# A fused sliding-window attention and mixer kernel: V of batch 1 ahead of the last quarter of w2, the four output sums of chunk 0 side by side, and unread matmuls between batch 0's values

## The chip, the cores and the metric

The kernel runs on one core of a Trainium2 chip. TensorE (PE, with its weight loads PEld) multiplies matrices into PSUM; VectorE (DVE), ScalarE (ACT) and GpSimd (POOL) work beside it, and SyncE (SP) issues transfers; POOL and ACT issue transfers too. The metric is the device time of one execution in microseconds. Lower is better.

## What is computed

Attention with a window of 64 over 8 batches, 8 heads, 576 positions and 64 dimensions a head; its output, laid out as (batch, position, 512), goes through a low-rank mixing of positions (U, V of rank 32) and a two-layer network with a relu. Types in and out are float32; the kernel computes in bf16 with float32 sums.

```python
scores = scale * np.matmul(q, k.transpose(0, 1, 3, 2))
mask = (rel >= 0) & (rel < window)            # rel = query position - key position
attn = softmax(np.where(mask, scores, -1e9))
x = np.matmul(attn, v)                        # then (B, S, H * D)
h = x.transpose(0, 2, 1) @ U @ V
u = x + h.transpose(0, 2, 1)
out = u + np.maximum(u @ w_ch1, 0.0) @ w_ch2
```

## The kernel before

**Work and tiles.** The 8 x 576 = 4,608 rows of u are cut into nine chunks of 512 rows for the network, while attention goes batch by batch. A chunk has 16 pieces `ch1(i)` (four matmuls of 128x512 into `psA`, then a relu on ScalarE or, for a few i, on VectorE) and 16 pieces `ch2(t, quarter)` (four matmuls of 128x512 into `psU`, the output sum of the 128 rows t; a quarter covers four of the sixteen row blocks of w2). After the last quarter of a t, the sum is added to u (line 683) and stored by SP. Each of these 32 pieces is the "fill" of one slot, 0 to 31.

Batch 0's attention runs alone, ahead of the loop. The attention of batch c + 1 is laid into the slots of chunk c: `KT` (transposes of K and Q on VectorE), `S` (scores on TensorE, exp on ScalarE at line 379, mask on VectorE at line 386), `VC` (copies that pair V's halves from `vA` into `vB`, lines 138 and 139), `PV` (values into `xr`, then reciprocal and multiply on VectorE, lines 417 and 427), `U` (into `pshh`, then a copy by ScalarE), `XT` and `UP` (the transposed u of the first two chunks, then four copies at line 551) and `V` (the addition of line 494). The tables `PLACE_1` and so on say which slot. In chunk 0, up to slot 20 the fill stands first and the slot's pieces behind it; from slot 21 on the pieces stand first. Within an engine everything runs in this written order.

**Order of the sums.** For chunk 0 the second layer goes by quarters over t = 0, 1, 2 and then takes t = 3 with all four quarters; other chunks go t by t.

**PSUM.** Pool `big` has two tiles of two banks, taken in turn by scores, values, U, XT and V. Pool `mm` has three tiles of one bank for `psA` and `psU`; pool `tp` has one tile of one bank, used for U of batch 1 only. In batch 0's stage a pool `x0` of two tiles stands in the place of `mm` and `tp`.

**Queues.** All loads from memory are issued by POOL, in this order around the change: w1 in three parts, w2 blocks 0 to 7, K and Q of batch 1 (four loads), w2 blocks 8 to 15, V of batch 1 (four loads into `vA`, one into `vB`), U for odd batches (two loads), then K and Q of batch 2 and V of batch 2 (lines 114 and 126 are the later batches' K, Q and V). The issues share eight completion semaphores in turn, so an issue waits until the eighth load before it has landed. SP stores the outputs and, with ACT and POOL, moves the transposed u of the later chunks.

**Unread matmuls.** `turn_over(n, cols)` multiplies a tile of zeros into a bank that nothing reads. It runs at the start, between score pieces of batch 0, and before chunk 0.

The lines that the change touches: 441 to 445 (bank of `pshh`), 671 and 672 (bank of a sum), 681 to 686 (emptying of a sum), 689 to 691 (order), `PLACE_1` (703 to 711), the loads (769 and 770) and batch 0's values (776 to 779).

Of the kernel before, what the change touches and what calls it, by code (L numbers as in the profile page):

```python
# [9 lines left out]
ALU = mybir.AluOpType  # L10

BF16 = mybir.dt.bfloat16
FP32 = mybir.dt.float32
# [3 lines left out]
def kernel(  # L17
# [11 lines left out]
    nc = tc.nc  # L29
# [93 lines left out]
    def load_v(b):  # L123
        va, vb = vA[b % 2], vB[b % 2]
        for t in range(NFULL):
            nc.gpsimd.dma_start(  # L126
                out=va[:, t, :, 0:D],
                in_=v[b, :, t * P : (t + 1) * P, :].rearrange("h p d -> p h d"),
            )
        nc.gpsimd.dma_start(  # L130
            out=vb[0:W, NFULL, :, 0:D],
            in_=v[b, :, NFULL * P : S, :].rearrange("h p d -> p h d"),
        )
# [65 lines left out]
    def load_w2(lo, hi):  # L199
        nc.gpsimd.dma_start(out=w2b[:, lo:hi, :], in_=w2v[:, lo:hi, :])  # L200
# [22 lines left out]
    def attention(b, alone=False):  # L223
# [213 lines left out]
        def UM(ts):  # L437
            def f():
                half = CH // 2
                if ts[0] == 0:  # L440
                    if b == 1:
                        hh["one"] = psum["tp"].tile([P, CH], FP32, name="pshh1", tag="tp")
                    else:
                        big = ps_big.tile([P, 2, CH], FP32, name="pshh", tag="big")
                        hh["one"] = big[:, 0, :]
                    if b < 2:
                        hh["ps"] = hh["one"].rearrange("p (n x) -> p n x", n=2)
                    else:
                        hh["ps"] = big[:, :, 0:half]
                ps = hh["ps"]  # L450
                for t in ts:
                    xt = x[:, t, :, :].rearrange("p h d -> p (h d)")
                    if b < 2:
                        nc.tensor.matmul(
                            hh["one"][t % 4 * R : (t % 4 + 1) * R, :],
                            ub[odd][:, t, :],
                            xt,
                            start=(t < 4),
                            stop=(t > 0),
                        )  # L460
                        continue
                    for n in range(2):
                        g = t if t < 4 else n
                        nc.tensor.matmul(
                            ps[g * R : (g + 1) * R, n, :],
                            ub[odd][:, t, :],
                            xt[:, n * half : (n + 1) * half],
                            start=(t < 4),
                            stop=(t != n),
                        )  # L470
                if ts[-1] == NT - 1:
                    hh["sb"] = wk_pool.tile([P, CH], BF16, name="hh", tag="hh")
                    nc.scalar.copy(out=hh["sb"].rearrange("p (n x) -> p n x", n=2), in_=ps)
            return f
# [133 lines left out]
    def mlp(c):  # L608
        uTc = uT_of(c)
        c1 = [None] * NFC  # L610

        psA0 = []

        def uT_cols(dc):
            cols = uTc[:, dc, :]
            if c < 2:
                return cols
            return cols.rearrange("p (i t q) -> p t i q", i=4, t=TPC)

        def ch1(i):  # L620
            def f():
                if c == 0 and i < 2:
                    if i == 0:
                        psA0.append(ps_big.tile([P, 2, CH], FP32, name="psA0", tag="big"))
                    ps = psA0[0][:, i, :]
                    todo = [(n, dc) for two in ((0, 2), (1, 3)) for n in range(2) for dc in two]
                else:
                    ps = psum["mm"].tile([P, CH], FP32, name="psA", tag="mm")[:]
                    todo = [(i, dc) for dc in range(NDC)]
                for n, dc in todo if c > 0 or i != 1 else ():  # L630
                    to = psA0[0][:, n, :] if c == 0 and n < 2 else ps
                    nc.tensor.matmul(  # L632
                        to if c < 2 else to.rearrange("p (t i q) -> p t i q", i=4, t=TPC),
                        w1b[:, dc, n * P : (n + 1) * P],
                        uT_cols(dc),
                        start=(dc == 0),
                        stop=(dc == NDC - 1),
                    )
                c1[i] = c1_pool.tile([P, CH], BF16, name=f"c1_{i}")
                if i in (DVE_RELU if c != 1 else (7, 10, 13)):  # L640
                    nc.vector.tensor_relu(out=c1[i][:], in_=ps)  # L641
                else:
                    nc.scalar.activation(out=c1[i][:], in_=ps, func=ACT.Relu)  # L643
            return f

        acc = {}

        def ch2(t, quarter):
            def f():
                g = c * TPC + t  # L650
                if c == NCH - 1 and t == TPC - 1:
                    if quarter % 2 == 0:
                        acc[t] = psum["mm"].tile([P, DM], FP32, name="psU", tag="mm")
                    cols = slice(quarter // 2 * (DM // 2), (quarter // 2 + 1) * (DM // 2))
                    for i in range(8 * (quarter % 2), 8 * (quarter % 2) + 8):
                        nc.tensor.matmul(  # L656
                            acc[t][:, cols],
                            c1[i][:, t * P : (t + 1) * P],
                            w2b[:, i, cols],
                            start=(i == 0),  # L660
                            stop=(i == NFC - 1),
                        )
                    if quarter % 2 == 1:
                        osb = out_pool.tile([P, DM], FP32, name="osb")
                        nc.vector.tensor_tensor(
                            out=osb[:, cols], in0=acc[t][:, cols], in1=u_tiles[g][:, cols], op=ALU.add
                        )
                        queue = nc.scalar if quarter == 1 else nc.sync
                        queue.dma_start(out=outf[g * P : (g + 1) * P, cols], in_=osb[:, cols])
                    return  # L670
                if quarter == 0:
                    acc[t] = psum["mm"].tile([P, DM], FP32, name="psU", tag="mm")
                for i in range(4 * quarter, 4 * quarter + 4):
                    nc.tensor.matmul(  # L674
                        acc[t][:],
                        c1[i][:, t * P : (t + 1) * P],
                        w2b[:, i, :],
                        start=(i == 0),
                        stop=(i == NFC - 1),
                    )  # L680
                if quarter == 3:
                    osb = out_pool.tile([P, DM], FP32, name="osb")
                    nc.vector.tensor_tensor(  # L683
                        out=osb[:], in0=acc[t][:], in1=u_tiles[g][:], op=ALU.add
                    )
                    nc.sync.dma_start(out=outf[g * P : (g + 1) * P, :], in_=osb[:])
            return f

        order = [(t, r) for t in range(TPC) for r in range(4)]
        if c == 0:  # L690
            order = [(t, r) for r in range(4) for t in range(3)] + [(3, r) for r in range(4)]
        return [ch1(i) for i in range(NFC)] + [ch2(t, r) for t, r in order]


# [7 lines left out]
    }  # L702
    PLACE_1 = {
        "KT": [11, 12, 14, 15],
        "S": [14, 14, 17, 17, 21, 21],
        "VC": [20, 21, 22, 23],
        "PV": [22, 23, 24, 25, 26],
        "U": [28],
        "XT": [28] * 4,
        "UP": [29],  # L710
    }
    PLACE_2 = {
        "V1": [0, 1, 17],
# [15 lines left out]
    def turn_over(n, cols=CH, to=None):  # L729
        for _ in range(n):  # L730
            nc.tensor.matmul(
                (unread if to is None else to)[:, 0, 0:cols],
                idle[:, 0:P],
                idle[:, 0:cols],
                start=to is None,
                stop=to is None,
            )
# [19 lines left out]
    for f in a["VC"][0:2]:  # L757
# [8 lines left out]
    load_w1(1024, 2048)  # L766
    load_w2(0, 8)
    load_kq(1)
    load_w2(8, 16)
    load_v(1)  # L770
    nc.gpsimd.dma_start(out=ub[1][W:P, 0, :], in_=moe_U[0:W, :])
    nc.gpsimd.dma_start(
        out=ub[1][:, 1:NT, :], in_=moe_U[W:S, :].rearrange("(c p) r -> p c r", p=P)
    )
    xT0 = [psum["x0"].tile([P, 2, CH], FP32, name=f"xT{i}", tag="x0") for i in range(2)]
    unread = xT0[0]
    a["PV"][2]()
    a["PV"][3]()
    a["PV"][4]()
    a["XT"][0]()  # L780
    for f in a["U"]:
# [95 lines left out]
```

## Time and profile before

| | us |
|---|---|
| median of four runs | 321.92 |
| lowest and highest of them | 320.49, 323.21 |
| the profiled execution's own time | 321.81 |
| its span, first to last instruction | 320.1 |
| TensorE matmuls busy, of the span | 308.9 (96%) |
| VectorE, ScalarE, GpSimd busy | 209.5, 106.1, 104.4 |

The profile is one execution. Busy time counts an engine's instructions, not its waits; matmuls overlap in the pipeline, so a busy TensorE isn't one at its peak. The clock row gives the share of full speed that TensorE was granted. Time outside the span (1.7 us here) belongs to the launch. Durations of one instruction that matter: a relu or copy of 128x512 out of PSUM on ScalarE, 597 ns; the sum's addition on VectorE, 671 ns; the exp of 128x768 on ScalarE, 811 ns; a copy of 64x520 on GpSimd, 616 ns, on ScalarE 621 to 625 ns, on VectorE some 290 ns. Matmuls of 128x512 start 0.216 us apart at full clock.

### The profile page before, as it was taken

The numbers are of one execution on the slowest core, as the hardware profiler recorded it, in microseconds if no ns is written. First come the engines' busy times: TensorE is split into PE (matmuls) and PEld (weight loads), VectorE is DVE, ScalarE is ACT, GpSimd is POOL, SyncE is SP. The second block draws the span as 40 slices with busy tenths as digits, with TensorE's granted clock in tenths as the row PEclk, the third lists the DMA queues.
The fourth block names the chain that finished last, engine by engine and source line by source line (L and its number), as shares of the span: only waits on it lengthen the run. The fifth ranks groups of instructions, "written<-read, shape, count | busy, mean of one in ns | idle before, by whom it ended". The sixth has DMA issues, their size and how long they took to land.

```text
span 320.1 us, 7020 instructions
## 1 busy us (share of the span) xinstructions
PE 308.9 (96%) x2879; PEld 152.1 (48%) x2905; DVE 209.5 (65%) x368; ACT 106.1 (33%) x174; POOL 104.4 (33%) x156
## 2 busy tenths in 40 slices
PE   8789998999999999999999999999999999999995
PEld 7554454455444544454444444444444444444444
DVE  7754948778797859778967795769577722412211
ACT  1544533275008320652065204630373004203400
POOL 8681428540059303930484038403000300030000
PEclk9979999999999999999999999999999999999999
DMA  7999999999359995999699939992400140050011
GB/s 118 160 194 206 207 152 165 206 194 126 28 144 165 161 79 131 146 167 124 147 168 175 85 62 192 184 131 38 165 0 2 41 158 0 0 166 33 2 66 67
DMA packets 108929, 38.05 MB, mean 119 GB/s; under 512 B 98352, under 2 KB 101808, under 8 KB 108896
## 3 DMA queue, kind: packets, MB, share of 16 engines
q0 software_dynamic: 92480, 25.63, 107.4%
q1 hardware_dynamic: 11232, 10.69, 10.1%
q10 hardware_dynamic: 5184, 1.28, 1.8%
q8 instruction: 23, 0.38, 0.5%
q14 instruction: 10, 0.08, 0.1%
HBM read 48.94 MB, written 9.44 MB: 182 GB/s over the span
## 4 chain that ended last, share of the span: by engine, by line
PE 61%; DMA 22%; POOL 6%; DVE 5%; issue 3%; SPq 2%; DVEq 0%; POOLq 0%
PE psA L632 27%; PE psU L674 26%; DMA vA<-in_v_dram 12%; DMA qr<-in_q_dram 5%; DMA w1b<-in_moe_w_ch_dram 3%; PE xr L408 2%; SPq L596 2%; PE sc L371 2%; POOL kr L114 2%; POOL qr L114 2%; DVE un L494 2%; PE psv L483 2%; DMA uTc<-stg 1%; DVE stg L570 1%; PE psU L656 1%
## 5 line engine op out<-in xcount | busy, mean ns | idle before, releaser
L632 PE MATMUL psA<-uTc,w1b 128*128 128x512 bf16 x570 | 132.5, 380 | 0.3
L674 PE MATMUL psU<-w2b,c 128*128 128x512 bf16 x542 | 125.7, 379 | 1.2 <-issue 0.3
L643 ACT ACTIVATE c<-psA 128x512 bf16<-128x512 f32 x101 | 60.3, 597 | 170.0 <-PE psA L632 170.0
L674 PEld LDWEIGHTS <-c 128*128 128x128 bf16 x560 | 53.6, 98 | 64.5 <-issue 1.9
L632 PEld LDWEIGHTS <-w1b 128*128 128x128 bf16 x576 | 53.5, 98 | 61.3 <-issue 0.2
L596 POOL DMA_DIRECT2D uTc<-stg x35 | 19.2, 558 | 115.2 <-DVE stg L570 76.3
L683 DVE TENSOR_TENSOR osb<-psU,un 128x512 f32<-128x512 f32 x35 | 23.5, 671 | 32.3 <-PE psU L674 32.2
L641 DVE TENSOR_SCALAR c<-psA 128x512 bf16<-128x512 f32 x43 | 29.5, 687 | 22.1 <-PE psA L632 20.5
L126 POOL DMA_DIRECT2D vA<-in_v_dram x32 | 28.4, 889 | 30.3 <-PE psA L632 9.9
L386 DVE TENSOR_TENSOR pts<-pts,mask 128x768 bf16<-128x768 bf16 x42 | 22.9, 556 | 18.6 <-ACT pts L379 16.2
L379 ACT ACTIVATE pts<-sc 128x768 bf16<-128x768 f32 x42 | 31.7, 811 | 3.8 <-PE sc L371 3.7
L494 DVE TENSOR_TENSOR un<-psv,xs 128x512 bf16<-128x512 f32 (+1 forms) x40 | 25.9, 674 | 10.0 <-PE psv L483 9.8
L427 DVE TENSOR_TENSOR xs<-xr,rcp 128x512 bf16<-128x512 f32 (+1 forms) x39 | 26.9, 691 | 1.3
L408 PEld LDWEIGHTS <-pts 128*64 128x64 bf16 x576 | 12.9, 111 | 12.9 <-DVE xs L427 5.9
L570 DVE STREAM_TRANSPOSE stg<-un 128x512 bf16<-128x512 bf16 x28 | 18.5, 683 | 0.0
L247 DVE STREAM_TRANSPOSE qt<-qr 128x576 bf16<-128x576 bf16 x20 | 15.7, 787 | 3.4 <-DMA vA<-in_v_dram 2.0
L114 POOL DMA_DIRECT2D kr<-in_k_dram x20 | 16.9, 844 | 3.1 <-DMA vA<-in_v_dram 1.9
L408 PE MATMUL xr<-vB,pts 128*64 128x65 bf16 x320 | 15.8, 197 | 1.8 <-ACT pts L330 0.8
L114 POOL DMA_DIRECT2D qr<-in_q_dram x20 | 17.0, 850 | 1.0 <-DMA vA<-in_v_dram 0.9
L247 DVE STREAM_TRANSPOSE kt<-kr 128x576 bf16<-128x576 bf16 x20 | 15.8, 789 | 1.5 <-DMA kr<-in_k_dram 1.5
L371 PEld LDWEIGHTS <-kt 64*64 64x64 bf16 (+1 forms) x720 | 10.1, 106 | 9.3 <-issue 8.7
L408 PE MATMUL xr<-vA,pts 128*64 128x65 bf16 x256 | 12.8, 196 | 0.8 <-DVE xs L427 0.8
(71 smaller groups left out, 159.8 us busy)
## 6 DMA issues: line engine op xcount, KB each, us to landing
out_dram<-osb SPq DMA_DIRECT2D x35, 256.0 KB, 2.6
kr<-in_k_dram POOLq DMA_DIRECT2D x26, 288.0 KB, 10.9
qr<-in_q_dram POOLq DMA_DIRECT2D x26, 288.0 KB, 12.1
vA<-in_v_dram POOLq DMA_DIRECT2D x32, 128.0 KB, 13.1
w2b<-in_moe_w_ch_dram POOLq DMA_DIRECT2D x2, 1024.0 KB, 18.9
uTc<-stg SPq DMA_DIRECT2D x42, 32.0 KB, 2.4
uTc<-stg ACTq DMA_DIRECT2D x35, 32.0 KB, 2.3
uTc<-stg POOLq DMA_DIRECT2D x35, 32.0 KB, 2.1
```

What stands on the lines that cost most here:

```text
L114: nc.gpsimd.dma_start(out=dst[32 * part : 32 * (part + 1), off : off + NJJ * RD].rearrange("p (n x) -> p n x", x=r * D), in_=src[b, m * NJ ...
L126: nc.gpsimd.dma_start(out=va[:, t, :, 0:D], in_=v[b, :, t * P : (t + 1) * P, :].rearrange("h p d -> p h d"),)
L247: nc.vector.transpose(out=dst[:, n * S : (n + 1) * S].rearrange("q (m p e) -> q m e p", p=32, e=r), in_=src[:, 32 + n * RD : 32 + (n + 1) ...
L379: nc.scalar.activation(out=dst, in_=sc[:, :, 0 : PB * W].rearrange("p g (n w) -> p g n w", w=W), func=ACT.Exp, scale=scale,)
L408: nc.tensor.matmul(xr[r0 : r0 + W, h // 4, (h % 4) * VW : (h % 4 + 1) * VW], pts[:, g, jj * NB + blk, :], rhs, start=True, stop=True,)
L427: nc.vector.tensor_tensor(out=x[lo:hi, t, :, :].rearrange("p (a h) d -> p a h d", a=2), in0=xv[:, :, :, 0:D], in1=rcp[lo:hi].to_broadcast( ...
L494: nc.vector.tensor_tensor(out=u_tiles[g][rs, :], in0=ps[rs, n, :], in1=xt[n][rs], op=ALU.add)
L596: queues[n % 3].dma_start(out=uT_of(c)[32 * j : 32 * (j + 1), :, i * run : (i + 1) * run], in_=stages[c][32 * i : 32 * (i + 1)].rearrange( ...
L632: nc.tensor.matmul(to if c < 2 else to.rearrange("p (t i q) -> p t i q", i=4, t=TPC), w1b[:, dc, n * P : (n + 1) * P], uT_cols(dc), start= ...
L641: nc.vector.tensor_relu(out=c1[i][:], in_=ps)
L643: nc.scalar.activation(out=c1[i][:], in_=ps, func=ACT.Relu)
L674: nc.tensor.matmul(acc[t][:], c1[i][:, t * P : (t + 1) * P], w2b[:, i, :], start=(i == 0), stop=(i == NFC - 1),)
```

## The change

The load of w2 blocks 8 to 15 is cut in two. Blocks 8 to 11 stay in their place, then come U's two loads, V of batch 1, and only then blocks 12 to 15. In chunk 0 the second layer goes by quarters over all four t, so that the last quarter of every sum comes in slots 28 to 31. The fourth sum of chunk 0 takes the bank of `tp`, and U of batch 1 takes a tile of `big`. Sums 0 and 1 of chunk 0 are copied by ScalarE and added to u by GpSimd in SBUF, in place of VectorE's one addition. Batch 1's pieces from the third pair of scores on move one slot earlier, V's copies too; `XT` stays in slot 28. Four unread matmuls of 128x512 are put ahead of the last three values of batch 0.

```diff
@@ UM
-                    if b == 1:
-                        hh["one"] = psum["tp"].tile([P, CH], FP32, name="pshh1", tag="tp")
-                    else:
-                        big = ps_big.tile([P, 2, CH], FP32, name="pshh", tag="big")
-                        hh["one"] = big[:, 0, :]
+                    big = ps_big.tile([P, 2, CH], FP32, name="pshh", tag="big")
+                    hh["one"] = big[:, 0, :]
@@ ch2
-                if quarter == 0:
+                if quarter == 0 and c == 0 and t == 3:
+                    acc[t] = psum["tp"].tile([P, DM], FP32, name="psU3", tag="tp")
+                elif quarter == 0:
                     acc[t] = psum["mm"].tile([P, DM], FP32, name="psU", tag="mm")
...
                     osb = out_pool.tile([P, DM], FP32, name="osb")
-                    nc.vector.tensor_tensor(
-                        out=osb[:], in0=acc[t][:], in1=u_tiles[g][:], op=ALU.add
-                    )
+                    if c == 0 and t < 2:
+                        nc.scalar.copy(out=osb[:], in_=acc[t][:])
+                        nc.gpsimd.tensor_tensor(
+                            out=osb[:], in0=osb[:], in1=u_tiles[g][:], op=ALU.add
+                        )
+                    else:
+                        nc.vector.tensor_tensor(
+                            out=osb[:], in0=acc[t][:], in1=u_tiles[g][:], op=ALU.add
+                        )
...
         if c == 0:
-            order = [(t, r) for r in range(4) for t in range(3)] + [(3, r) for r in range(4)]
+            order = [(t, r) for r in range(4) for t in range(TPC)]
@@ PLACE_1
         "KT": [11, 12, 14, 15],
-        "S": [14, 14, 17, 17, 21, 21],
-        "VC": [20, 21, 22, 23],
-        "PV": [22, 23, 24, 25, 26],
-        "U": [28],
+        "S": [14, 14, 17, 17, 20, 20],
+        "VC": [19, 20, 21, 22],
+        "PV": [21, 22, 23, 24, 25],
+        "U": [27],
         "XT": [28] * 4,
-        "UP": [29],
+        "UP": [28],
@@ loads
     load_kq(1)
-    load_w2(8, 16)
-    load_v(1)
+    load_w2(8, 12)
     nc.gpsimd.dma_start(out=ub[1][W:P, 0, :], in_=moe_U[0:W, :])
     nc.gpsimd.dma_start(
         out=ub[1][:, 1:NT, :], in_=moe_U[W:S, :].rearrange("(c p) r -> p c r", p=P)
     )
+    load_v(1)
+    load_w2(12, 16)
...
     unread = xT0[0]
+    turn_over(1)
     a["PV"][2]()
+    turn_over(2)
     a["PV"][3]()
+    turn_over(1)
     a["PV"][4]()
```

## The prediction

> **What bounds the kernel now.** I read the page's rows by slice first, then the chain of waits, then the timeline of the first 65 us, then the DMA view. The page's rows, 40 slices of 8 us:
>
> ```profile
> span 320.1 us, 7020 instructions
> ...
> PE   8789998999999999999999999999999999999995
> ...
> PEclk9979999999999999999999999999999999999999
> DMA  7999999999359995999699939992400140050011
> ```
>
> From about 62 us on TensorE is a closed stream: spacing its matmul starts, I find no wait of weight but the usual 0.09 us at a change of operation. Whatever starts that stream later or earlier moves the end by as much, and the change edits nothing behind it except which engine empties two sums. So the sum is made in the first 62 us, in three places.
>
> Place 1, the clock. Two stretches as the clock cuts them (PE, PEld, DVE, ACT, POOL busy, granted clock, DMA share, GB/s):
>
> ```profile
> 14.28:17.70 3.42, 1.71 (x59) 1.20 (x53) 2.54 (x8) 3.20 (x11) 2.32 (x5) 1.00 1.50 180
> 17.70:21.11 3.41, 3.41 (x28) 2.12 (x29) 1.69 (x4) 0.91 (x3) 3.41 (x7) 0.50 1.20 183
> ```
>
> After a half-idle stretch (batch 0's values, waiting for V's copies) the clock is halved for 3.41 us, while batch 0's transposes, U and part of UP run.
>
> Place 2, the first scores of batch 1, from the timeline (start, us):
>
> ```profile
> 33.97 0.67 DVE L494 TENSOR_TENSOR un<-psv,xs 64x512 bf16<-64x512 f32 x1
> ...
> 34.57 1.24 DVE L239 STREAM_TRANSPOSE kt<-kr 128x576 uint32<-128x576 uint32 x1
> ...
> 35.86 1.26 DVE L239 STREAM_TRANSPOSE qt<-qr 128x576 uint32<-128x576 uint32 x1
> ...
> 37.17 0.76 PE L371 MATMUL sc<-qt,kt 32*64 32x128 bf16 x48 [0.17 <-DVE qt L239]
> ```
>
> TensorE waits here for a transpose of Q, and that transpose starts 0.03 us after its data: the first Q load of batch 1, issued at 19.38, takes 16.4 us (DMA view; its landing event is at 35.83). K's landed at 34.46. Two transposes, a relu, two masks and the last transpose then follow on VectorE without a gap to 41.03, where the second pair of scores takes it. The DMA row says why: the queue is full from 2 us on and drains in order.
>
> Place 3, batch 1's values, the only large wait of TensorE:
>
> ```profile
> 44.94 1.51 ACT L379 ACTIVATE pts<-sc 128x768 bf16<-128x768 f32 x2 [1.90 <-PE sc L371]
> ...
> 45.27 0.81 PE L674 MATMUL psU<-w2b,c 128*128 128x512 bf16 x3 [0.16 <-issue]
> ...
> 46.01 0.45 PE L408 MATMUL xr<-vB,pts 128*64 128x65 bf16 x8
> ...
> 46.87 0.29 DVE L138 COPY vB<-vA 64x520 bf16<-64x520 bf16 x1 [1.20 <-DMA vA<-in_v_dram]
> ...
> 47.51 1.03 DVE L386 TENSOR_TENSOR pts<-pts,mask 128x768 bf16<-128x768 bf16 x2
> ...
> 48.81 0.69 DVE L427 TENSOR_TENSOR xs<-xr,rcp 64x512 bf16<-64x512 f32 x1
> ...
> 49.56 0.22 PE L408 MATMUL xr<-vA,pts 128*64 128x65 bf16 x1 [0.79 <-DVE xs L427]
> ```
>
> V's second piece lands at 46.84; VectorE, held by its copy, only then masks the last scores and empties PV 0, so PV 2 starts at 49.56. The last matmul before it started at 48.40 and needs 0.22, the change of operation 0.09: TensorE lost **0.85 us**.
>
> **Part by part.**
>
> *Unread matmuls.* Four of 128x512 at 0.216 (the spacing of psA). They wait for the exp that last read their bank (ends 16.06). The first fills the hole before PV 2 (16.18) and makes it some 0.14 late; two delay PV 3 by 0.43, to 17.1, but PV 4 waits for VectorE's emptying of PV 2 anyway (17.60, started 17.70); the fourth falls before that. So they cost the path at most 0.1. Do they keep the clock? The streamed columns of 14.28:17.70 are 3,380, at 2.4 columns per ns 41% of it; 2,048 more make 66%. The next stretch, halved, held 5,000 and was followed by full clock. Here the Trainium skill speaks against the change: "TensorE: Matmul & The Clock Gate", in "HAM oscillation", asks only that TensorE have no idle gap over about 3.4 us. The row disagrees: the largest gap before the drop was 0.77 us, and the drop came; it is the share of a stretch that counted. By the rule the matmuls are needless and bring nothing; by the row they restore the clock. Then 8 of PV 4, 16 of XT and 5 of U run at full rate; U's last matmul still waits for VectorE (19.46). U then ends some 0.27 earlier, XT saves 12 x 0.05, so UP starts about 0.65 earlier, less the 0.1: chunk 0's ch1 starts **0.55 earlier**, at 22.1.
> It is lost at place 2. TensorE reached the scores 0.24 before it could start them (the last matmul before them starts at 36.62; plus 0.22 and 0.09 is 36.93); now it will be there 0.8 before. The first Q load is issued before anything that the change moves, so qt stays at 35.86 and the scores at 37.17; VectorE's closed row fixes the second pair too. Contribution: 0, whatever the clock does within 0.24 us of today. What else might be late with ch1 earlier is not: w1's last half lands at 27.95, ch1 8 needs it at about 29.5.
>
> *V of batch 1.* POOL's DMAs use eight completion semaphores in turn, so each issue waits for the landing of the eighth before it. POOL's queue now holds w2 rows 8-12, two small U loads, five of V, w2 12-16, then K and Q of batch 2. V's five are issued later than before (33.3 to 39.6, not 23.3 to 36.8: the landings of w2's first half at 33.01 and of the four K and Q loads to 38.62 free them), but still ahead of the moment when the queue reaches them. The w2 load of 1024 KB took 43.70 - 38.62 = 5.08; half of it 2.54; the U loads 0.17 each. So V comes 2.54 - 0.34 = **2.2 us earlier**: its pieces at 42.8, 44.65, 45.75, 46.8, 47.3. The second rule weighed: "DMA: Bandwidth & Descriptors", in the anatomy of the SWDGE path, fits 2.0 us + bytes/436e3 for each DMA, so that one DMA more would eat 2.0 of the 2.2. In the trace the four loads of 288 KB land 1.4 apart, less than 2.0 in all: queued loads pay nothing fixed. By the rule the forecast would be that of rival C; I take the row.
> With V's second piece at 44.65, its copies end at 45.3, before the exp of the last scores. Place 3's wait goes: **-0.85**, if nothing else is late.
>
> *Batch 1's pieces one slot earlier.* Something else is. Up to slot 20 a slot's fill stands ahead of its pieces, from 21 behind. Before, scores 2 and 5 (slot 21) were followed by four psU, then PV 0. Now they end slot 20 and PV 0 opens slot 21: nothing between. Both banks of "big" hold scores; PV 0 takes the first when its exp has read it: 44.94 + 0.81 (mean of L379) = 45.75, start 45.80. TensorE is free at 45.05. **A new wait of 0.75.** Then PV 0 and a fill repeat every 1.35 (46.01 to 47.35): PV 1 at 47.15, PV 2 at 48.50. PV 2's needs: the exp of scores 5 ends at 46.45, masks to 47.0, reciprocal and multiply to 47.95; ScalarE's copy of V's third piece 46.5-47.1. Nothing is late; PV 3 (49.85) and 4 (51.2) neither. Against before: PV 2 is 1.06 earlier, but one fill (0.86 + 0.09) is moved behind it: **-0.1**.
>
> *All four sums, last quarter last.* The same 64 psU matmuls. The fourth sum takes the bank of "tp"; U's sum moves to "big" (free after PV 3; its copy, 0.6 on ScalarE, lies beside the fill of slot 27, 0.86; without that cover, up to 0.6). w2's last quarter is issued when its first part lands (41.2) and lands near 49.7; it is needed at about 57. After UP (57.1) sixteen psU take 3.46, to 60.5. ch1 0 and 1 of chunk 1 need sums 0 and 1 emptied: ScalarE, 58.1-58.7 and 59.0-59.6 (0.60, row L643), cover 1.7 and over. ch1 2 needs sum 2: VectorE at 60.5 for 63.0. VectorE in order (uT, kt, osb, qt, osb, un) ends un at 64.8, as before, when batch 2's scores ask for it. GpSimd's two additions have no row; its copy of 64x520 takes 0.62, VectorE's addition of this size 0.67. Between 0.6 and 2.5 for one, only the store and the issue of V of batch 3 (65.5 before, wanted after 100) stand behind them: 0.
>
> **Sum.** 0 - 0.85 + 0.75 = -0.1: span 320.0. The profiled execution took 321.81, 1.7 beyond its span and 0.1 below the median of 321.92: **321.7 us**.
>
> **Rivals.**
> B: *the exp wait doesn't show, or the clock's gain survives.* For it: ScalarE is idle for 1.9 before that exp. Against: TensorE must write those scores first. -0.85 gives 320.9; with the 0.55 of the clock as well, 320.4.
> C: *V is not earlier*, slower. The chain landing, copies, masks, emptying, PV 2 takes 49.56 - 46.84 = 2.72; PV 2 is ready at 48.50, so the second piece must land by 45.8, 1.1 after my estimate. At 46.8 PV 2 starts at 49.56 as before, with one fill more behind it: +0.86, 322.7.
> D: *the unread matmuls move the halving instead of lifting it*, for instance to 21.1-24.5: ch1 loses 1.7 of work, less 0.55 + 0.24: +0.9, 322.7. Against: the stretch that would decide it already passed at 5,000 columns.
>
> **How the numbers follow.** Forecast 0.6, B 0.2, C 0.1, D 0.05, unforeseen 0.05. No change means within 0.5% (1.6 us), what a measurement of this kernel can tell; all four named cases lie inside it. With the spread of the runs shown (320.49 to 323.21) about a third of B and half of the unforeseen pass it downward, a third of C and D and the rest upward: faster 0.12, same 0.79, slower 0.09. The range takes in B and C and stops at 320.1 and 322.9.
>
> **What would show it.** Right: clock 1.00 at 17.7-21.1, ch1 0.5 earlier, yet the first scores of batch 1 again near 37.2 behind qt; V's second piece near 44.7; PV 0 waiting about 0.75 for the exp of L379; ch1 of chunk 1 within 0.3 of before. Wrong: an earlier landing of K and Q of batch 1, V's second piece after 45.8, or a wait of ch1 0 to 2 of chunk 1 for a bank.

## The result, and the profile after

| | median us (lowest to highest, runs) | ratio, 95% interval |
|---|---|---|
| before | 321.17 (319.73 to 323.57, 59) | |
| changed | 323.41 (320.89 to 327.55, 38) | 1.0057 [1.0043, 1.0071] |

The changed kernel is 0.57% slower, some 1.8 us, where 321.7 us and no change were forecast. The medians hold all executions; the ratio leaves out those over 1.5% above the fastest of their kernel, six of the changed kernel's 38 and its first profiled one (326.08 us, with the clock halved for 3.41 us at 222 us). The lines of the profile after are therefore those of a second profiled execution of the same kernel, of 321.86 us (the run `e0_again` below). That one is the fastest of its 15, and its span is that of before (320.1), so it shows less than the whole loss.

From its page, the rows that answer to those of before, and one of the costliest groups (busy, mean ns of one, then idle time before it and its releaser):

```profile
span 320.1 us, 7059 instructions
...
PE   8899989999999999999999989999999999999995
...
PEclk9989999999999999999999999999999999999999
DMA  6999999999759995999499939996500240050011
...
q8 instruction: 23, 0.38, 0.6%
...
L480 PE MATMUL psv<-hh,vrep 128*128 128x512 bf16 x40 | 12.6, 380 | 1.0 <-DVE un L491 1.0
```

One group is new among the costliest: TensorE's addition of V (L480; L483 before) waits for VectorE's `un`. It falls in the attention of a later batch. The page of the first profiled execution says the same with more time:

```profile
L480 PE MATMUL psv<-hh,vrep 128*128 128x512 bf16 x39 | 12.3, 379 | 3.9 <-DVE un L491 3.9
```

**The head**, where the whole forecast was made. Scores and values of batch 1 in the second execution, from the timeline (start, us, engine, line, count; in brackets the idle time before and what ended it):

```profile
36.05 1.22 DVE L239 STREAM_TRANSPOSE qt<-qr 128x576 uint32<-128x576 uint32 x1
...
37.32 0.76 PE L371 MATMUL sc<-qt,kt 32*64 32x128 bf16 x48
...
44.38 0.29 DVE L138 COPY vB<-vA 64x520 bf16<-64x520 bf16 x1
...
44.47 0.80 PE L371 MATMUL sc<-qt,kt 32*64 32x64 bf16 x56
45.96 0.42 PE L408 MATMUL xr<-vB,pts 128*64 128x65 bf16 x8 [0.69 <-ACT pts L379]
...
48.63 0.22 PE L408 MATMUL xr<-vA,pts 128*64 128x65 bf16 x1
```

V's second piece is copied at 44.38, not at 46.87. PV 2 starts at 48.63 without a wait, not at 49.56. PV 0 has the new wait for the exp, 0.69. Chunk 1 begins at 60.5, before at 60.6. So the head went nearly as forecast, and the time was lost behind it.

**Where it was lost.** The wait of L480 lies in chunk 4. The waits between 150 and 190 us (engine, line, what it waited for: us, times, longest), first of before, then of the changed kernel's two executions:

```profile
POOL hold L581 <- DMA uTc<-stg: 1.9, 1, 1.9
DVE qt L247 <- DMA qr<-in_q_dram: 1.4, 1, 1.4
...
PE psv L483 <- DVE un L494: 0.4, 1, 0.4
DVE kt L247 <- DMA kr<-in_k_dram: 0.4, 1, 0.4
```

```profile
POOL hold L578 <- DMA uTc<-stg: 4.2, 1, 4.2
DVE qt L247 <- DMA vA<-in_v_dram: 1.5, 1, 1.5
...
PE psv L480 <- DVE un L491: 1.0, 1, 1.0
DVE kt L247 <- DMA kr<-in_k_dram: 0.9, 1, 0.9
```

```profile
POOL hold L578 <- DMA uTc<-stg: 4.8, 1, 4.8
...
DVE kt L247 <- DMA kr<-in_k_dram: 1.7, 1, 1.7
PE psv L480 <- DVE un L491: 1.7, 1, 1.7
```

Read them from the top. `hold` is a tiny copy on GpSimd that waits for the last of the 16 moves of u for chunk 4 (`uTc<-stg`) and lets the loads of K and Q of batch 6 follow. It waits 2.3 us longer; some 0.8 of that isn't the moves, since `hold` waits 2.7 in the changed kernel even where they take 5.5 us (`e1_no_unread`, below). VectorE then waits longer for K (0.9 for 0.4), `un` comes later, and TensorE waits. The chain is already in before, with 0.4 us at its end: the loop from moves to loads to transposes to moves was only just in time there.

What stands beside the late moves is a transfer that the kernel doesn't issue. Queue q8 of the page (kind "instruction") has 23 pieces, 0.38 MB; by their number they are TensorE's own instructions, fetched as the kernel runs (the count is in the last section). In the transfers between 155.5 and 157.5 us of the second execution stands

```profile
q8 instruction: 1, 0.02, 5.0%
```

that is, of 16 engines and 2 us, one piece of 1.6 us. It came at 156.1, inside the moves (first issue 153.0, last landing 160.1: 7.1 us). In before the piece came at 161.0, after the moves (153.1 to 158.6: 5.5 us). The same view of before has no such line between 155.5 and 157.5 us, and this one between 160.5 and 162.5:

```profile
q8 instruction: 1, 0.02, 3.0%
```

The experiments ask whether this is the cause.

### The profile page after: what moved, and what is told of

The parts are those of the page before. It is cut to its first block, busy times and chain, and to the rows that moved or that the text cites. A ratio compares the mean times of both kernels' runs of the same rounds, so it can differ in the third digit from the quotient of the medians.

```text
span 324.4 us, 7032 instructions
## 1 busy us (share of the span) xinstructions
PE 310.1 (96%) x2882; PEld 152.1 (47%) x2909; DVE 208.3 (64%) x366; ACT 107.2 (33%) x176; POOL 107.7 (33%) x159
## 4 chain that ended last, share of the span: by engine, by line
PE 62%; DMA 19%; POOL 6%; DVE 5%; issue 3%; SPq 2%; ACT 1%; DVEq 0%; POOLq 0%; ACTq 0%
PE psU L673 28%; PE psA L629 25%; DMA qr<-in_q_dram 14%; PE xr L408 3%; DMA vA<-in_v_dram 3%; PE sc L371 2%; POOL kr L114 2%; SPq L593 2%; DMA uTc<-stg 2%; DVE un L491 2%; PE psv L480 2%; POOL qr L114 2%; DVE stg L567 1%; ACT pts L379 1%; PE psU L653 1%
## 5 line engine op out<-in xcount | busy, mean ns | idle before, releaser
L673 PE MATMUL psU<-w2b,c 128*128 128x512 bf16 x543 | 127.7, 383 | 1.0 <-issue 0.2
L640 ACT ACTIVATE c<-psA 128x512 bf16<-128x512 f32 x101 | 60.3, 597 | 174.3 <-PE psA L629 174.3
L688 DVE TENSOR_TENSOR osb<-psU,un 128x512 f32<-128x512 f32 x33 | 22.1, 670 | 33.9 <-PE psU L673 33.8
L567 DVE STREAM_TRANSPOSE stg<-un 128x512 bf16<-128x512 bf16 x28 | 18.5, 684 | 0.0
L480 PE MATMUL psv<-hh,vrep 128*128 128x512 bf16 x39 | 12.3, 379 | 3.9 <-DVE un L491 3.9
## 6 DMA issues: line engine op xcount, KB each, us to landing
kr<-in_k_dram POOLq DMA_DIRECT2D x26, 288.0 KB, 11.2
qr<-in_q_dram POOLq DMA_DIRECT2D x26, 288.0 KB, 12.4
```

The lines of the kernel that those rows point to most:

```text
L673: nc.tensor.matmul(acc[t][:], c1[i][:, t * P : (t + 1) * P], w2b[:, i, :], start=(i == 0), stop=(i == NFC - 1),)
```

## The experiments

**First group: the parts, one at a time.** Which part of the change carries the loss: the unread matmuls, the order of the loads, or the way the sums are emptied? `e0_again` is the changed kernel as it is.

> The changed kernel once more, for its profile and a ratio taken beside the other runs of this batch. Theory late loads: the first 62 us are as forecast (the first ch1 of chunk 1 within 0.5 us of before or earlier), and the loss of 1 to 2 us arises behind 150 us, where K and Q of a later batch land after VectorE asks for them; ratio 1.004 to 1.007. Theory head: the loss is already there at 62 us (ch1 of chunk 1 at 61.5 or later).

1.0076 [1.0051, 1.0100].

`e1_no_unread`: the changed kernel without its four unread matmuls.

```diff
-    turn_over(1)
     a["PV"][2]()
-    turn_over(2)
     a["PV"][3]()
-    turn_over(1)
     a["PV"][4]()
```

> The changed kernel without the four unread matmuls. Theory late loads, set off by the shifted instruction stream (eight more rows on TensorE move every later instruction fetch): back near before, ratio 0.996 to 1.002. Theory late loads, set off by the order of loads or by stores: ratio stays 1.004 to 1.007. Theory head: within 0.1 us of the changed kernel.

1.0018 [0.9990, 1.0046]: most of the loss is gone. The waits of the same window have no wait of TensorE for `un` left:

```profile
POOL hold L578 <- DMA uTc<-stg: 2.7, 1, 2.7
DVE qt L247 <- issue: 0.5, 1, 0.5
```

`e2_old_loads`: the changed kernel with the loads in the order of before.

```diff
-    load_w2(8, 12)
+    load_w2(8, 16)
+    load_v(1)
     nc.gpsimd.dma_start(out=ub[1][W:P, 0, :], in_=moe_U[0:W, :])
...
-    load_v(1)
-    load_w2(12, 16)
```

> The changed kernel with the order of loads of before (w2 blocks 8 to 15 whole, V of batch 1, then U). Theory late loads, set off by the load order (one load more, all later loads on the next semaphore): ratio back to 0.998 to 1.003, with V's second piece at 46.8 and the value wait of 0.9 back in the head. Otherwise the ratio gets worse, about 1.007 to 1.010, as V's gain of 0.9 us is given up.

1.0103 [1.0070, 1.0136]: no better, and by its middle 0.27% worse than `e0_again`, with intervals that overlap. The new order of loads is not the loss.

`e3_vector_empties`: all four sums emptied by VectorE's one addition.

```diff
-                    if c == 0 and t < 2:
-                        nc.scalar.copy(out=osb[:], in_=acc[t][:])
-                        nc.gpsimd.tensor_tensor(
-                            out=osb[:], in0=osb[:], in1=u_tiles[g][:], op=ALU.add
-                        )
-                    else:
-                        nc.vector.tensor_tensor(
-                            out=osb[:], in0=acc[t][:], in1=u_tiles[g][:], op=ALU.add
-                        )
+                    nc.vector.tensor_tensor(
+                        out=osb[:], in0=acc[t][:], in1=u_tiles[g][:], op=ALU.add
+                    )
```

> The changed kernel with all four sums of chunk 0 emptied by VectorE as before, none by ScalarE and GpSimd; stores then go out near 60 us and not at 65. Theory late loads, set off by the four stores that now run beside the loads of batch 3: ratio back to 0.998 to 1.002. Otherwise ratio 1.004 to 1.008, a little worse for a wait of the first ch1 pieces of chunk 1 for their banks (0 to 1 us).

1.0055 [1.0033, 1.0078]: still slower. The engine that empties two sums is not the loss either.

What is left is the four unread matmuls. They lie at 16 to 18.5 us, and the loss at 184. The three profiles here that have 2,909 weight loads on their page, and the first one of the changed kernel, all had the piece of q8 inside the moves of chunk 4; `e1_no_unread`, with 2,905 as before, did not. So the new theory: not where the matmuls stand, but that TensorE's stream is eight instructions longer (a weight load and a matmul each; the "rows" in the names of the next runs are these instructions).

**Second group: the length of the stream alone.** The warm-up at the start has 70 small unread matmuls whose number is of no matter otherwise. `f1_before_plus_rows` is the kernel before with four more of them, the edit shown; `f3_before_minus_rows` has four fewer, 66:

```diff
-    turn_over(70, W)
+    turn_over(74, W)
```

> The kernel before with four more unread matmuls of 64 columns in the warm-up at the very start, where TensorE waits for its first data anyway: TensorE has the eight extra rows of the changed kernel (5820, not 5812) and nothing else of it. Theory instruction fetch: the fetch of TensorE's next 16 KB that stood at 161 us moves to about 156, into the moves of u for chunk 4 (from 153), which then take 7 us and not 5.5; K and Q of the batch behind them are issued 1.5 us later, TensorE waits 0.9 to 1.5 at 184; ratio 1.004 to 1.007. Theory of the other parts (load order, emptying, slots): ratio 0.999 to 1.001, fetch and moves unchanged.

> The kernel before with four unread matmuls fewer in the warm-up (5804 rows). Theory instruction fetch: the fetch stays behind the moves of u for chunk 4 (at 161 or a little later) and the ratio is 0.998 to 1.002; if it fell into other moves, its place will be seen. Theory of the other parts: 0.999 to 1.001. This one tells whether any change of rows hurts, or only one that brings the fetch into the moves.

`f2_after_rows_restored` is the changed kernel, unread matmuls and all, with four fewer in the warm-up:

```diff
-    turn_over(70, W)
+    turn_over(66, W)
```

> The changed kernel whole, with four unread matmuls of 64 columns fewer in the warm-up, so that TensorE's row count is that of before (5812). Theory instruction fetch: fetch back near 160.5, moves of u for chunk 4 in 5.5 us, ratio 0.996 to 1.002. Theory that the four unread matmuls hurt where they stand (path or clock): ratio stays 1.005 to 1.008.

The kernel before with eight instructions more is slower by as much as the changed kernel: 1.0083 [1.0050, 1.0116]. The changed kernel with eight fewer is back: 1.0003 [0.9981, 1.0025]. Eight fewer in the kernel before change nothing: 0.9996 [0.9976, 1.0017]. In `f1_before_plus_rows` the waits read like those of the changed kernel, though none of its parts is there:

```profile
POOL hold L581 <- DMA uTc<-stg: 3.9, 1, 3.9
...
PE psv L483 <- DVE un L494: 2.0, 1, 2.0
DVE kt L247 <- DMA kr<-in_k_dram: 1.9, 1, 1.9
```

`g1_rows_and_fill_behind_scores` is `f2_after_rows_restored` with slot 20 of chunk 0 turned round, so that a fill stands between the last scores and PV 0.

```diff
-            early = c == 0 and n > 20
+            early = c == 0 and n > 19
```

> The changed kernel with the row count restored and, in chunk 0, slot 20 too with its pieces ahead of its fill, so that four matmuls of the second layer stand between the last scores of batch 1 and its first values. Forecast's step on the exp wait: the 0.75 us in front of the first values goes, 0.6 to 0.75 us less than with the rows alone restored, ratio 0.994 to 0.999. Theory that only the load loop of the middle chunks sets the end: no difference from the rows alone restored.

0.9997 [0.9976, 1.0018]. The wait for the exp is gone, as the timeline shows (the bracket before the fill is time in which TensorE waited for nothing that the profile shows; PV 0 has none), and chunk 1 begins at 59.7, not 60.1; yet the time is that of `f2_after_rows_restored`, as far as intervals of some 0.7 us to either side can tell.

```profile
44.44 0.81 PE L673 MATMUL psU<-w2b,c 128*128 128x512 bf16 x3 [0.16 <-issue]
45.18 0.45 PE L408 MATMUL xr<-vB,pts 128*64 128x65 bf16 x8
```

**Third group: is it `hold` that passes the delay on?** If the late moves cost time only because `hold` keeps the loads back, then without `hold` the eight instructions should cost nothing. The three kernels leave out the copies of `next_loads`, so that the loads of K and Q no longer wait for the moves: `h1_rows_no_hold` is `f2_after_rows_restored` so, `h2_changed_no_hold` the changed kernel, `h3_rows_fill_no_hold` is `g1_rows_and_fill_behind_scores`.

```diff
         def f():
-            for i, j in last_pieces[c + 1]:
-                rows = slice(32 * j, 32 * (j + 1))
-                nc.gpsimd.tensor_copy(
-                    out=hold[rows, 0:1], in_=uT_of(c + 1)[rows, 0, i * TPC * 32 : i * TPC * 32 + 1]
-                )
             load_kq(c + 3)
```

> The changed kernel with the row count restored, and without the small GpSimd copies (tile hold) that make the next loads of K and Q wait until the moves of u have landed. Theory load loop (moves land, K and Q are issued, land 21 us later, their transposes hold back the next moves): K and Q are issued about 3.5 us earlier in every chunk, the wait near 217 goes, ratio 0.990 to 0.997 if the moves keep under 8.5 us; if the loads slow the moves past the chunk's start, TensorE waits there and the ratio is 1.005 or more. Theory that the loop does not set the end: ratio as with the rows restored, 1.000.

> The changed kernel with its 5820 rows, without those copies. Theory instruction fetch through the load loop: the fetch still falls near 156 and still slows the moves, but K and Q no longer wait for them, so the loss behind 180 us goes: ratio within 0.002 of the same with restored rows. Theory that the extra rows cost by themselves, not through the loads: 0.006 to 0.008 above it.

> The changed kernel with restored rows, with the fill between the last scores of batch 1 and its first values, and without those copies. If the load loop is cut, what the head gains is kept: 0.6 to 0.75 us less than without the fill, ratio 0.988 to 0.996. If not, no difference from the one without the fill.

1.0137 [1.0088, 1.0185], 1.0282 [1.0241, 1.0322] and 1.0104 [1.0065, 1.0143]: all three slower, and the eight instructions cost more here, not nothing. For `h1_rows_no_hold` it is the second case of its expectation, TensorE waiting at the start of chunks 2 to 5 (1.2 us at most). Whether `h3_rows_fill_no_hold` keeps what the head gains isn't shown, since the first and the last interval overlap. Without `hold` the loads run beside the moves, which for chunk 4 take 8.2, 11.9 and 8.4 us, and TensorE waits for them at the start of the chunks. In `h2_changed_no_hold` the piece of q8 comes on top of that (at 158.5, inside the moves; in the other two at 168.7, behind them); TensorE waits over 4 us, and the clock row has a second dip, in slice 20:

```profile
PEclk9989999999999999999969999999999999999999
```

So the removal of `hold` opens another, dearer way for the same delay. `hold` as the only carrier is refuted; in these profiles late moves cost time on either way.

`h4_before_unread_alone`: the kernel before with the four unread matmuls in their place and four fewer in the warm-up. It asks what the unread matmuls do to the clock when the stream keeps its length.

```diff
-    turn_over(70, W)
+    turn_over(66, W)
...
+    turn_over(1)
     a["PV"][2]()
+    turn_over(2)
     a["PV"][3]()
+    turn_over(1)
     a["PV"][4]()
```

> The kernel before with the four unread matmuls between batch 0's values, and four fewer in the warm-up, so that TensorE's row count is that of before. Forecast's step: the clock stays full at 17.7 to 21.1, ch1 of chunk 0 starts 0.5 us earlier, and the first scores of batch 1 wait for Q's transpose as before: ratio 0.998 to 1.002. Theory that the unread matmuls hurt in place: 1.005 or more.

1.0006 [0.9989, 1.0023]: nothing gained, nothing lost.

**All of them side by side**, without the three that have no `hold`. The number of weight loads is that of the page; fetch is the piece of q8 near the moves of chunk 4, the moves run from their first issue to the last landing, chunk 4 is the time from its first `psA` to that of chunk 5, and the last column is TensorE's wait for `un` in it (a dash: none over 0.15 us), all from the one profiled execution of each.

| kernel | weight loads | ratio | span | fetch | moves | chunk 4 | wait for `un` |
|---|---|---|---|---|---|---|---|
| before | 2,905 | | 320.1 | 161.0 | 5.5 | 33.5 | 0.4 |
| e1_no_unread | 2,905 | 1.0018 | 318.4 | 160.4 | 5.6 | 32.9 | - |
| f2_after_rows_restored | 2,905 | 1.0003 | 319.3 | 160.3 | 5.5 | 33.0 | - |
| g1_rows_and_fill_behind_scores | 2,905 | 0.9997 | 319.0 | 159.9 | 5.5 | 32.9 | - |
| h4_before_unread_alone | 2,905 | 1.0006 | 319.4 | 161.3 | 5.5 | 33.0 | - |
| f3_before_minus_rows | 2,901 | 0.9996 | 320.9 | 161.2 | 5.5 | 33.1 | - |
| e0_again | 2,909 | 1.0076 | 320.1 | 156.1 | 7.1 | 34.1 | 1.0 |
| e2_old_loads | 2,909 | 1.0103 | 321.8 | 156.9 | 7.5 | 34.4 | 1.3 |
| e3_vector_empties | 2,909 | 1.0055 | 321.8 | 156.9 | 7.0 | 34.5 | 1.4 |
| f1_before_plus_rows | 2,909 | 1.0083 | 322.5 | 156.8 | 7.5 | 35.1 | 2.0 |

The rows fall into two sets with nothing between them, in the fetch, in the moves, in the ratio and in both columns of chunk 4. The spans of the four long ones are 2.0 us longer in the mean (321.55 against 319.52). Of that, 1.4 lies in chunk 4 (34.5 against 33.1), 0.5 before chunk 1 (60.9 against 60.3) and 0.2 in chunks 1 to 3; chunk 5 gives 0.2 back. There the same wait stands in both sets (up to 0.7 in the long ones, 0.4 in before, 1.4 in `f3_before_minus_rows`), so it doesn't part them. From chunk 6 to the end it is 91.9 us in every one.

## Why the prediction was wrong, step by step

**The step that failed** is the one that the sum stood on: "From about 62 us on TensorE is a closed stream: spacing its matmul starts, I find no wait of weight", and from it "the change edits nothing behind it except which engine empties two sums. So the sum is made in the first 62 us". Both halves were wrong.

*It was not closed.* The timeline of before has, at 184.97, the 0.40 us that I took for small:

```profile
180.82 0.82 DVE L247 STREAM_TRANSPOSE qt<-qr 128x576 bf16<-128x576 bf16 x1 [1.42 <-DMA qr<-in_q_dram]
...
184.97 0.39 PE L483 MATMUL psv<-hh,vrep 128*128 128x512 bf16 x1 [0.40 <-DVE un L494]
```

A second such wait, of 0.39, stands at 218.50, in chunk 5. A wait of 0.40 costs little, but it says that the slack of the loop behind it is nil: K and Q of batch 6 are issued when the moves have landed (159.3), need until 180.7, and VectorE waits for them. A later landing of the moves is passed on until it reaches TensorE. The page of before hinted at it in its chain of waits, the view that I read second: DMA has 22% of the chain and TensorE only 61%.

```profile
PE 61%; DMA 22%; POOL 6%; DVE 5%; issue 3%; SPq 2%; DVEq 0%; POOLq 0%
```

I used that view for the head alone. A chain with 28% of DMA and GpSimd in it was a reason to look behind 62 us: from 153 to 218 us it runs through moves, loads and transposes. The share measures no loss, though: in `e0_again`, which is slower, TensorE has 87% and DMA 6%.

*The change edits what lies behind.* Four unread matmuls make TensorE's stream eight instructions longer, and every later piece of it is fetched at another place in the program. I had counted their time on TensorE (0.1 us) and their columns for the clock, not the instructions themselves. In the second execution the moves landed 1.5 us later, K and Q of batch 6 were issued 1.5 us later (160.8 against 159.3) and the last of them landed 0.5 later (181.2 against 180.7); TensorE's wait grew by about as much, from 0.4 to 1.0. In the first execution it was 1.7. `f1_before_plus_rows` and `f2_after_rows_restored` show that this length decides, each against its pair. With the length restored the ratio is what was forecast, 1.0003, though not by the forecast's sum: the head gained more than it said, and waits further on remained. Rival D had blamed the same matmuls, but for the clock; this cause was among none of the rivals.

**The other steps.**

- *V of batch 1, 2.2 us earlier:* right. Its second piece landed at 44.35, not 46.84, so 2.5 earlier. The rule of 2.0 us for each DMA (the Trainium skill, "DMA: Bandwidth & Descriptors", in the anatomy of the SWDGE path), read as a price that queued loads pay one after the other, would have made the four V loads land at least 2.0 apart; they landed 1.9, 1.0 and 1.0 apart, and the two small loads of U 0.2 each. The row was the right choice.
- *A new wait of 0.75 for the exp:* right, 0.69, and 0.70 in `e1_no_unread`.
- *The unread matmuls keep the clock:* right in some executions only, and by the wrong rule. In the second execution the clock was halved all the same, before and over them (the columns as in the prediction's fence; PEclk is the first number after the five engines):

```profile
15.50:18.91 3.41, 3.15 (x43) 1.37 (x36) 1.65 (x7) 2.05 (x9) 2.90 (x5) 0.50 1.42 189
```

  The halving began at 15.50, the first unread matmul at 15.86; in `h4_before_unread_alone` they lie at 16.41 and 15.71. In the 3.41 us before 15.50 TensorE was busy for 2.38 us (1.71 before the halving of before), with no gap over 0.45. So neither the share of a stretch, from which I argued, nor the skill's rule of idle gaps over 3.4 us ("TensorE: Matmul & The Clock Gate") tells when it falls here. In the first execution of the changed kernel the head had no halving at all. How often that is, the granted clocks of all executions tell: one halving of 3.41 us in 320 takes the mean to 0.995 (an estimate from these two numbers). Of 154 executions of kernels with the four matmuls 63 have 0.998 or more; of 146 without them (before, e1, f1 and f3) none is above 0.995. So they spare the halving in some four of ten, and what decides stays open. To the time it is worth nothing that shows: `h4_before_unread_alone` has 1.0006, and its nine executions at 0.998 or more took 322.0 us in the mean, the other thirteen 321.7.
- *Place 2, Q holds the scores at 37.17:* half right. In the second execution the scores started at 37.32 with no wait, since TensorE itself was later; in the first they waited 0.23 for Q, at 36.73. In `e1_no_unread` Q landed at 35.02 and they started at 36.65. I had taken the landing for fixed; over the profiles here it lay between 35.0 and 36.2.
- *Chunk 1 within 0.3 us of before (60.6):* 60.5 and, in the first execution, 59.9; 59.8 in `e1_no_unread`. So in single executions the head of the change is worth up to 0.8 us, more than I gave it. That shows in no ratio: `f2_after_rows_restored` and `g1_rows_and_fill_behind_scores` lie at 1.0003 and 0.9997, with intervals of some 0.7 us to either side. Their profiles have a wait of 0.6 at 217 us in the same group (psv for un). That the loop of loads takes the gain away there is read from these single executions, and not tested by itself.
- *The sums at nothing:* nothing speaks against it: `e3_vector_empties` has 1.0055 against 1.0076, with overlapping intervals.
- *Rival C's price of 0.86 us* for V not earlier: `e2_old_loads` is 0.27% above `e0_again`, 0.9 us, but the intervals overlap, so it isn't shown.

**What stays open.** That moves with a fetch inside them take longer is shown below. That the late moves are what costs the time is read from the profiles (table above); the three runs meant to cut that link (h1 to h3) opened another. Why eight instructions move this fetch by 5 us and not by their own 1 or 2 is only argued: in the short streams of the table it comes 0.2 to 0.5 us before the first `psA` of chunk 4, which waits for the moves, and in the long ones 5 us before it. That fits a sequencer that reads ahead until an instruction has to wait, with the border of a piece just before or just behind that instruction. No run tested it, and two profiles don't fit it as it stands: without `hold`, in `h1_rows_no_hold` and `h3_rows_fill_no_hold`, which have 2,905 too, the fetch came 4.9 and 4.5 us behind that `psA`. Some 0.7 of the 2.0 us lie before chunk 4, and I have no cause for them.

## What to carry to other kernels

A small wait late in a stream, with a transfer at the end of its chain, marks a loop without slack: before calling a stream closed, ask what it would pass on. Instructions that do nothing still lengthen an engine's stream and move its later fetches; when some are added, take as many out of a place where they don't matter, or run the unchanged kernel with the same number added, and only then judge what they were added for.

## What the hardware did that I had not expected

**Instruction fetches meet the kernel's own transfers.** TensorE's stream came in 23 pieces of 16,384 bytes, each taking 0.9 to 2.3 us. The Trainium skill, "Runtime: NRT & Kernel Launch", section "Instruction fetch mechanics", gives 16 KiB blocks of 256 instructions and calls the cost of a border "mostly hidden". The size agrees with the trace (0.38 MB by 23, and 23 times 256 is just over the 5,818 weight loads and matmuls). Hidden it was for TensorE (in before its only idle times over 0.15 us behind chunk 0 are the two waits for `un`), but not for the moves. The eleven profiled executions with `hold` have 77 sets of 16 moves: the 20 sets with a fetch of q8 inside took 6.5 to 7.7 us, the 57 without 5.4 to 5.8, with none between. The last set alone shows it too: in before, with a fetch at 284.0, it took 6.7 us, and in `f3_before_minus_rows`, where that fetch came at 288.0, behind them, 5.5 us.

How one fetch delays 16 transfers is only seen from outside. The rows below, from the transfers between 150 and 165 us, are GB/s in slices of 0.375 us, first of `e1_no_unread`, then of the second execution of the changed kernel:

```profile
GB/s 11 17 20 17 9 0 0 0 0 0 169 94 103 198 143 181 120 153 154 43 77 350 399 388 372 388 164 71 70 71 111 145 176 165 134 140 111 132 143 145
```

```profile
GB/s 96 51 35 41 27 19 17 10 5 0 0 89 168 94 172 137 240 105 144 87 5 10 13 90 3 87 268 393 361 404 371 301 4 94 90 85 67 81 143 219
```

Above, the moves run through from 153.8 to 157.9, and the stores (over 300) follow at once. Below, after 157.5 there are five slices, 1.9 us, with little moved (5, 10, 13, 90, 3), although moves are outstanding: they land at 160.1. The hole opens as the fetch, 156.1 to 157.7, ends; why, no run shows.
